# Row maxima ahead of the value and weight loads, fillers in two slots, second weight scale one slot later

## The chip, the cores and the metric

The kernel runs on one core of a Trainium2 chip. Its five engines work side by side, each through its own queue in order: TensorE (PE) multiplies matrices, VectorE (DVE) and ScalarE (ACT) work on elements, GpSimd (POOL) works on elements and issues DMAs, and SyncE (SP) issues DMAs. The metric is the device time of one execution in microseconds (us). The kernel before takes 1290.05 us in the median of three runs (1287.4 to 1290.46).

## The reference

The program is block-causal attention, and its output goes through a feed-forward layer with a gate.

```
scores = scale * np.matmul(q, k.transpose(0, 1, 3, 2))      # 8 x 8 heads of 576 x 64
scores = np.where(block_i >= block_j, scores, -1000000000.0)  # blocks of 64
attn = np.exp(scores - max); attn = attn / (sum + 1e-09)
x = (attn @ v).transpose(0, 2, 1, 3).reshape(4608, 512)
h = x @ w_in                                                 # 512 -> 2048
g = h * erf(softplus(h))
out = g @ w_out                                              # 2048 -> 512
```

## The kernel before

There are 64 heads, eight to a batch, and the program goes through them in slots (L648). Slot n makes the probabilities of head n (`probs`, L431: scores transposed as tile t, two matmuls to a piece, exponentials on ScalarE), the row maxima of head n + 2 (`maxes`, L387: scores as tile s on TensorE, six maxima on VectorE), and loads head n + 3 (`load_qk`, L371). The maxima of a head are turned on TensorE (tile mt, L424), copied by ScalarE and sent by a small DMA into one row of that head's `qk` tile (L427); the first matmul of the head's probabilities (L440) waits for that DMA. Every second slot multiplies the probabilities of two heads by v (`pv`, tile u) and sums their rows (tile us); every fourth slot normalises four heads (`normalise`) and sends the result x to memory.

`qk` takes four buffers. Each has five further rows with the mask, loaded once from `maskrows`. A head's load is three DMAs, two of them on POOL's queue and one on SP's, and then two subtractions on POOL (L382, L383) that make the low halves. The staging tile `st` of that load has two buffers.

The weights come as 64-bit floats, 32 half pieces of 512 KB, each 128 x 1024 words (`load_raw`, two buffers), and are converted by `to_f32`: two ScalarE passes and three VectorE passes a piece. Sixteen of the pieces are group 0 of the layer, sixteen are group 1. `TOF` says in which slots pieces are converted, `SCALE_AT` in which slot a group's scale is taken, and `SPLIT` in which slots its eight tiles are split into two half-precision parts. The layer's matmuls (m_h at L185 up, o at L194 down) begin when batch 0 is normalised, x has been read back and group 0 is split. From then on `moe1` gives out one step at a time, 12 a slot up to slot 19 and 28 a slot from slot 20.

Until the layer has read its first x, each slot also issues ten matmuls of a constant tile, whose result nobody reads (`warm`, L645): the fillers. Code order is not the final order. A scheduler places the instructions on each engine by priority, and the rows in the section on the change show what it made.

Of the kernel before, what the change touches and what calls it, by code (L numbers as in the profile page):

```python
# [23 lines left out]
def f32(ap):  # L24
    return ap.bitcast(F32)
# [7 lines left out]
def tile_attention_moe(ctx: ExitStack, tc: tile.TileContext, qk, v, w, maskrows, sels, out):  # L33
    nc = tc.nc
    B, H, D4, S = qk.shape
    D = D4 // 4
    NT, DM = out.shape
    NF = w.shape[0]
    P = 128
    NCC = DM // P  # L40
    SCALE = 0.125
    NQ = H // 4
# [19 lines left out]
    ident = cpool.tile([P, P], F32, name="ident")  # L62
    make_identity(nc, ident)
    ones32 = cpool.tile([P, 32], F16, name="ones32")
    nc.gpsimd.memset(ones32, 1.0)
    ones32t = cpool.tile([P, 32], F16, name="ones32t")
    nc.gpsimd.memset(ones32t, 0.0)
    nc.gpsimd.memset(ones32t[: S % P], 1.0)
    ones = cpool.tile([P, P], F32, name="ones")
    nc.gpsimd.memset(ones, 1.0)  # L70
# [35 lines left out]
    def load_raw(f, s, pool):  # L106
        raw = pool.tile([P, 2 * DM], I32, tag="raw", name=f"raw{f}_{s}", bufs=2)
        nc.sync.dma_start(raw, w[f, s].bitcast(I32))
        return raw.rearrange("p (n t) -> p n t", t=2)
# [179 lines left out]
    with tc.tile_pool(name="apool", bufs=2) as apool, tc.tile_pool(name="spool", bufs=1) as spool, \  # L289
# [5 lines left out]
        def memsets():  # L295
            nc.gpsimd.memset(pstage[0][64:128, 768:], 0.0)
            for t in rss:
                nc.gpsimd.memset(t[64:, S - SH :], 1.0)
            for t in mxs:
                nc.gpsimd.memset(t, 0.0)  # L300
# [13 lines left out]
        def load_v(b, qd):  # L314
            vt = apool.tile([P, 2, 4, 5, D], F16, tag="v", name=f"v{b}_{qd}")
            if b < B32:
                v32 = f32(vt.rearrange("p a b c d -> p (a b c d)")).rearrange("p (a b) -> p a b", a=4)
            else:
                v32 = apool.tile([P, 4, 5 * D], F32, tag="v32", name=f"v32_{b}_{qd}", bufs=1)
            nc.sync.dma_start(v32, v[b, :, 4 * qd : 4 * qd + 4, :])  # L320
            return v32, vt
# [257 lines left out]
        lows = []  # L579
        normals, ready_at, ready = {}, {}, 0  # L580
        for n in range(NB - 1):
            load, low = load_qk(n)
            if n == 2:
                for f in lows:
                    f()
                lows = []
            load()
            lows.append(low)
            nc.gpsimd.dma_start(qks[n][D : D + 5, 2 * S : 4 * S], maskrows)
            if n == 0:  # L590
                v32 = load_v(0, 0)
            if n == 1:
                memsets()
        nc.gpsimd.dma_start(qks[NB - 1][D : D + 5, 2 * S : 4 * S], maskrows)
        sel = spool.tile([P, 4], F32, name="sel")
        nc.sync.dma_start(sel, sels)
        for low in lows:
            low()
        scale_v(0, 0, *v32)
        vs[0] = prep_v(0, 0, *v32)  # L600
        rows = {}
        for n in range(2):
            *steps, rows[n] = maxes(n)
            for f in steps:
                f()
        rows.pop(0)()
# [11 lines left out]
        HALVES = [(f, i) for f in range(NF) for i in range(2)]  # L618
        TOF = {1: 2, 2: 2, 3: 2, 4: 2, 5: 2, 6: 2, 7: 2, 8: 2} | {n: 2 for n in range(11, 19)}
        SCALE_AT = {9: 0, 19: 1}  # L620
        SPLIT = {9: 2, 10: 3, 11: 3, 19: 2, 20: 2, 21: 2, 22: 2}
        raws = {}

        def next_raw():
            if len(raws) < len(HALVES):
                fs = HALVES[len(raws)]
                raws[fs] = load_raw(*fs, apool)

# [19 lines left out]
        for n in range(N + 3):  # L648
# [12 lines left out]
            qd = n // 4 + 1  # L661
            if n % 4 == 1 and qd < N // 4:
                v32 = load_v(*divmod(qd, NQ))
# [26 lines left out]
            if not loaded:  # L690
                lists.append(([warm] * WARM, 0, 1))
# [44 lines left out]
```

## Time and profile before

| | us |
|---|---|
| median of three runs | 1290.05 |
| the profiled execution | 1288.4 |
| its span | 1286.6 |
| TensorE busy | 1200.5 (93%) |
| VectorE busy | 895.8 (70%) |
| ScalarE busy | 780.5 (61%) |
| GpSimd busy | 523.6 (41%) |

The profile is one execution. Its page gives sums, and the trace behind it gives every instruction with its start, its duration, and the idle time before it with what ended it. Sums over the whole span say little of one stage: the first 165 us hold loads, conversions and attention alone, and after that the layer's matmuls fill TensorE. The granted clock is told as a share of full speed, 1.00 or 0.50 at any moment, so that 0.58 in a stretch is a mean of the two.

### The profile page before, as it was taken

What the parts mean: (1) busy time and instruction counts of PE and PEld (TensorE: products, weight loads), DVE (VectorE), ACT (ScalarE), POOL (GpSimd) and SP (SyncE); (2) the same over time, 40 slices, a digit from 0 to 9 for tenths busy, and PEclk for the clock granted to TensorE, in tenths of its full rate; (3) what the DMA queues carried; (4) which work ended last, traced back from release to release, by engine and by line L of the source; (5) the groups of instructions that cost most, each with busy time, mean ns of one, the idle gap of its engine ahead of it and who ended that gap; (6) DMA issues with size and microseconds to landing.
All of it is one profiled execution on the core that took longest, in us unless ns stands there. A gap on an engine that the chain in (4) does not pass through costs nothing.

```text
span 1286.6 us, 23640 instructions
## 1 busy us (share of the span) xinstructions
PE 1200.5 (93%) x9108; PEld 810.2 (63%) x9108; DVE 895.8 (70%) x1583; ACT 780.5 (61%) x1555; POOL 523.6 (41%) x488
## 2 busy tenths in 40 slices
PE   1899999989999999999999999999999999999997
PEld 0455566556666666767667666766667667666664
DVE  3853689887567878688777778795777765555554
ACT  2453567667556666766666756666666775555553
POOL 4444435553435453545445344544445331321221
PEclk9887889989999999999999999999999999999999
DMA  9794566862454554453545444554444221221111
GB/s 250 210 218 97 125 170 172 229 148 67 109 122 121 135 133 110 105 143 114 110 114 124 111 109 128 131 122 100 115 112 113 63 69 52 82 66 50 53 63 50
DMA packets 95808, 151.74 MB, mean 118 GB/s; under 512 B 7804, under 2 KB 44988, under 8 KB 95696
## 3 DMA queue, kind: packets, MB, share of 16 engines
q1 hardware_dynamic: 69840, 93.34, 24.4%
q0 software_dynamic: 25216, 56.73, 21.5%
q8 instruction: 72, 1.18, 0.4%
q14 instruction: 40, 0.33, 0.1%
q10 hardware_dynamic: 640, 0.17, 0.1%
HBM read 121.73 MB, written 28.31 MB: 117 GB/s over the span
## 4 chain that ended last, share of the span: by engine, by line
PE 49%; DVE 26%; ACT 14%; DMA 5%; issue 4%; POOL 1%; SPq 0%; DVEq 0%; POOLq 0%; ACTq 0%
PE m_h L185 14%; PE o L194 14%; DVE m_r L158 5%; DVE m_r L157 5%; PE u L489 4%; DVE m_r L159 4%; DVE m_r L160 3%; PE t L440 3%; ACT m_r L155 3%; ACT m_r L154 3%; PE s L394 3%; ACT m_r L156 3%; PE t L441 3%; DVE mx L397 2%; PE us L512 2%
## 5 line engine op out<-in xcount | busy, mean ns | idle before, releaser
L185 PE MATMUL m_h<-xh,w 128*128 128x256 f16 x2304 | 476.9, 276 | 12.8 <-DVE m_r L160 12.5
L185 PEld LDWEIGHTS <-w 128*128 128x128 f16 x3456 | 326.7, 99 | 146.6 <-issue 24.1
L194 PE MATMUL o<-w,m_gh 128*128 128x512 f16 x1152 | 337.0, 382 | 10.5 <-DVE pt L235 6.4
L162 POOL TENSOR_TENSOR m_gl<-m_r,m_gh 128x512 f16<-128x512 f32 x144 | 174.3, 1211 | 403.6 <-ACT m_gh L161 362.8
L185 PE MATMUL m_h<-xl,w 128*128 128x256 f16 x1152 | 316.6, 275 | 0.0
L397 DVE TENSOR_REDUCE mx<-s 64x1 f32<-64x288 f32 (+4 forms) x384 | 174.8, 470 | 110.8 <-PE s L394 109.8
L157 DVE SCALAR_TENSOR_TENSOR m_r<-m_r 128x512 f32<-128x512 f32 x144 | 115.6, 803 | 171.1 <-ACT m_r L156 168.9
L445 ACT ACTIVATE p<-t 128x288 f32<-128x288 f32 (+4 forms) x384 | 146.0, 385 | 108.7 <-PE t L441 102.7
L194 PE MATMUL o<-w,m_gl 128*128 128x512 f16 x576 | 206.0, 384 | 0.3 <-POOL m_gl L162 0.3
L161 ACT CAST m_gh<-m_r 128x512 f16<-128x512 f32 x144 | 88.8, 617 | 192.0 <-DVE m_r L160 187.9
L440 PE MATMUL t<-qk 69*128 69x288 f32 (+4 forms) x384 | 168.0, 438 | 13.1 <-DMA qk<-mt 7.5
L394 PE MATMUL s<-qk 68*64 68x288 f32 (+3 forms) x384 | 150.9, 424 | 27.4 <-DVE mx L397 14.9
L382 POOL TENSOR_TENSOR qk<-st,qk 64x576 fp32r<-64x576 f32 x64 | 95.9, 1498 | 149.4 <-DMA qk<-qk 136.2
L154 ACT ACTIVATE m_r<-m_h,c,bs 128x512 f32<-128x512 f32 (+3 forms) x192 | 124.1, 666 | 45.1 <-PE m_h L185 43.0
L194 PEld LDWEIGHTS <-m_gh 128*128 128x128 f16 x1152 | 98.5, 98 | 67.2 <-issue 19.7
L158 DVE SCALAR_TENSOR_TENSOR m_r<-m_r,m_r 128x512 f32<-128x512 f32 x144 | 120.6, 837 | 2.8
L441 PE MATMUL t<-qk 128*128 128x288 f32 (+4 forms) x384 | 120.1, 313 | 0.0
L159 DVE SCALAR_TENSOR_TENSOR m_r<-m_r 128x512 f32<-128x512 f32 x144 | 115.7, 803 | 2.9
L383 POOL TENSOR_TENSOR qk<-st,qk 64x576 fp32r<-64x576 f32 x64 | 103.1, 1611 | 30.0 <-DMA qk<-qk 27.1
L457 DVE TENSOR_TENSOR p<-p,p 128x832 f16<-128x832 f32 x80 | 82.6, 1033 | 36.3 <-ACT p L456 36.2
L156 ACT ACTIVATE m_r<-m_r,c 128x512 f32<-128x512 f32 x144 | 103.7, 720 | 2.9 <-ACT m_r L155 0.8
L155 ACT ACTIVATE m_r<-m_r,c 128x512 f32<-128x512 f32 x144 | 103.8, 721 | 1.7
(98 smaller groups left out, 1484.9 us busy)
## 6 DMA issues: line engine op xcount, KB each, us to landing
qk<-qk POOLq DMA_DIRECT2D x64, 432.0 KB, 5.0
st<-qk SPq DMA_DIRECT2D x64, 288.0 KB
qk<-qk POOLq DMA_DIRECT2D x64, 288.0 KB, 5.2
raw<-w SPq DMA_DIRECT2D x32, 512.0 KB
v<-v SPq DMA_DIRECT2D x16, 640.0 KB
x_d<-xs POOLq DMA_DIRECT2D x32, 288.0 KB, 3.5
xh<-x_d SPq DMA_DIRECT2D x36, 256.0 KB
xl<-x_d SPq DMA_DIRECT2D x36, 256.0 KB
```

Source lines behind the costliest of these rows:

```text
L154: nc.scalar.activation(r0s[:, :, lo:hi], h[:, :, lo:hi], AF.Tanh, bias=const(p1), scale=bss[b][g][:, 0:1])
L157: nc.vector.scalar_tensor_tensor(out=r0, in0=r0, scalar=c3, in1=r0, op0=ALU.add, op1=ALU.mult)
L158: nc.vector.scalar_tensor_tensor(out=r0, in0=r1, scalar=c4, in1=r0, op0=ALU.add, op1=ALU.mult)
L159: nc.vector.scalar_tensor_tensor(out=r0, in0=r0, scalar=c5, in1=r0, op0=ALU.add, op1=ALU.mult)
L162: nc.gpsimd.tensor_tensor(out=gl, in0=r0, in1=gh, op=ALU.subtract)
L185: nc.tensor.matmul(h[:, k, :], lhsT=wf[:, a, sl], rhs=x[:, cc, :], start=cc == 0 and i == 0, stop=cc == NCC - 1 and i == 2)
L194: nc.tensor.matmul(o[c], lhsT=a[:, sl], rhs=wf[:, b_, :], start=u == u0 and k == 0 and not lo and b_ == 2, stop=u == u1 - 1 and k == nu - ...
L394: nc.tensor.matmul(dst[:r, :w_], lhsT=qh[:K, i * P : i * P + r], rhs=kh[:K, k0 : k0 + w_], start=True, stop=True)
L397: nc.vector.tensor_reduce(out=mx[:r, col : col + 1], in_=src, axis=AX.X, op=ALU.max, negate=True)
L440: nc.tensor.matmul(s[:kk, :w_], lhsT=kh[:K, ks], rhs=qh[:K, q0 : q0 + w_], start=True, stop=False)
L441: nc.tensor.matmul(s[:kk, :w_], lhsT=klh[:, ks], rhs=qhl[:, q0 : q0 + w_], start=False, stop=True)
L445: nc.scalar.activation(p32s[part][:kk, c : c + w_ - skip], s[:kk, skip:w_], AF.Exp, scale=SCALE)
```

## The change

- The mask rows are loaded once from memory, first on POOL's queue, and copied into the other three buffers by DMAs on ScalarE's queue. Their masked value is -2^100 in place of -1e30.
- Heads 0 to 2 are loaded next. The constants are set after head 1's load has been issued, the memsets after head 2's.
- The first load of v, and the loads of the first weight pieces, now wait: VectorE writes one element from the row maxima into the target tile, and the load, which overwrites that element, stands behind it. Later loads of v have such a copy too.
- The first v is scaled in slots 0 and 1. One piece of weights is converted in each of slots 0 and 1, then two a slot up to slot 8 as before.
- Fillers stand in slots 0 and 1 alone.
- The second scale is taken in slot 20 in place of 19, and the eight tiles of group 1 are split in slots 20 to 23 in place of 19 to 22.

```
+        if src is not None:
+            nc.vector.tensor_copy(f32(raw[:1, :1]), src)
         nc.sync.dma_start(raw, w[f, s].bitcast(I32))
...
+            nc.vector.tensor_copy(v32[:1, 0, :1], src)
             nc.sync.dma_start(v32, v[b, :, 4 * qd : 4 * qd + 4, :])
...
+        heads = [load_qk(n) for n in range(NB - 1)]
+        masks = [qks[n][D : D + 5, 2 * S : 4 * S] for n in range(NB)]
+        nc.gpsimd.dma_start(masks[0], maskrows)
+        for m in masks[1:]:
+            nc.scalar.dma_start(f32(m), f32(masks[0]))
+        heads[0][0]()
         sel = spool.tile([P, 4], F32, name="sel")
         nc.sync.dma_start(sel, sels)
+        heads[1][0]()
+        constants()
+        heads[2][0]()
+        memsets()
+        for _, low in heads:
             low()
-        scale_v(0, 0, *v32)
-        vs[0] = prep_v(0, 0, *v32)
...
         for n in range(2):
             *steps, rows[n] = maxes(n)
             for f in steps:
                 f()
-        rows.pop(0)()
+            if n == 0:
+                v32 = load_v(0, 0, mxs[0][:1, 3:4])
+                rows.pop(0)()
+            next_raw(mxs[n][:1, 3:4])
...
-        TOF = {1: 2, 2: 2, 3: 2, 4: 2, 5: 2, 6: 2, 7: 2, 8: 2} | {n: 2 for n in range(11, 19)}
-        SCALE_AT = {9: 0, 19: 1}
-        SPLIT = {9: 2, 10: 3, 11: 3, 19: 2, 20: 2, 21: 2, 22: 2}
+        TOF = {0: 1, 1: 1, 2: 2, 3: 2, 4: 2, 5: 2, 6: 2, 7: 2, 8: 2} | {n: 2 for n in range(11, 19)}
+        SCALE_AT = {9: 0, 20: 1}
+        SPLIT = {9: 2, 10: 3, 11: 3, 20: 2, 21: 2, 22: 2, 23: 2}
...
+            if n < 2:
+                lists.append(([lambda v0=v32: scale_v(0, 0, *v0), lambda v0=v32: vs.__setitem__(0, prep_v(0, 0, *v0))][n : n + 1], 0.6, 0.8))
             if n % 4 == 1 and qd < N // 4:
-                v32 = load_v(*divmod(qd, NQ))
+                v32 = load_v(*divmod(qd, NQ), mxs[(n + 1) % 2][:1, 3:4])
...
-            if not loaded:
+            if n < 2:
                 lists.append(([warm] * WARM, 0, 1))
...
-        maskrows[j, 1, 128 * j : 128 * j + 64] = -1e30
+        maskrows[j, 1, 128 * j : 128 * j + 64] = -(2.0**100)
```

VectorE at the start of the program, before: its first maxima (mx, from the scores s of heads 0 and 1) stand behind the conversion of the first pieces of weights (w from raw, the pieces of tiles 1 and 2 shown).

```order
L116 TENSOR_SCALAR w_99<-raw_0_371 128x512
L117 SCALAR_TENSOR_TENSOR w_99<-a_0_478,w_99 128x512
L118 SCALAR_TENSOR_TENSOR w_99<-a_0_478,w_99 128x512
L116 TENSOR_SCALAR w_99<-raw_1_484 128x512
L117 SCALAR_TENSOR_TENSOR w_99<-a_1_486,w_99 128x512
L118 SCALAR_TENSOR_TENSOR w_99<-a_1_486,w_99 128x512
L116 TENSOR_SCALAR w_100<-raw_0_492 128x512
L117 SCALAR_TENSOR_TENSOR w_100<-a_0_575,w_100 128x512
L116 TENSOR_SCALAR w_100<-raw_1_581 128x512
L397 TENSOR_REDUCE mx_152<-s_0_207 128x1 x2
```

VectorE at the same place now, from its first instruction on:

```order
L403 TENSOR_REDUCE mx_144<-s_0_200 128x1 x2
L403 TENSOR_REDUCE mx_144<-s_0_205 128x1
L403 TENSOR_REDUCE mx_144<-s_0_208 128x1
L403 TENSOR_REDUCE mx_144<-s_0_0_211 64x1
L403 TENSOR_REDUCE mx_144<-s_0_1_214 64x1
L325 COPY v_0_217<-mx_144 1x1
L112 COPY raw_0_226<-mx_144 1x1
L428 TENSOR_REDUCE mx_144<-mx_144 64x1
```

The maxima of head 0 are VectorE's first work, and the two copies behind them release the loads of v and of the first piece of weights.

SP's queue at the start, before (st: a head's staging tile, v, raw: a piece of weights):

```order
L378 DMA st_170<-qk 128x576
L320 DMA v_0_175<-v 128x1280
L378 DMA st_177<-qk 128x576
L596 DMA sel<-sels 128x4
L320 DMA v_1_316<-v 128x1280
L108 DMA raw_0_355<-w 128x1024
L108 DMA raw_1_363<-w 128x1024
L320 DMA v_3_0_3154<-v 128x1280
L108 DMA raw_0_371<-w 128x1024
L108 DMA raw_1_484<-w 128x1024
```

SP's queue at the start now:

```order
L384 DMA st_162<-qk 128x576
L593 DMA sel<-sels 128x4
L384 DMA st_163<-qk 128x576
L384 DMA st_164<-qk 128x576
L384 DMA st_250<-qk 128x576
L326 DMA v_0_217<-v 128x1280
L113 DMA raw_0_226<-w 128x1024
L113 DMA raw_1_246<-w 128x1024
L384 DMA st_326<-qk 128x576
L113 DMA raw_0_375<-w 128x1024
```

Four heads' staging loads now stand ahead of v, and pieces of weights alternate with heads.

TensorE in slot 7, before (t: probabilities of head 7, s: scores of head 9, mt: maxima of head 8, warm: the fillers):

```order
L440 MATMUL t_7_0_992<-qk_137 128x288
L441 MATMUL t_7_0_992<-qk_137 128x288
L394 MATMUL s_9_996<-qk_135 128x256 x2
L645 LDWEIGHTS ones_82
L645 MATMUL warm<-ones_82 32x512
L440 MATMUL t_7_288_1002<-qk_137 128x288
L441 MATMUL t_7_288_1002<-qk_137 128x288
L645 LDWEIGHTS ones_82
L645 MATMUL warm<-ones_82 32x512
L394 MATMUL s_9_1007<-qk_135 128x384
L424 MATMUL mt_1011<-ident,mx_152 5x128
```

TensorE in slot 7 now:

```order
L446 MATMUL t_7_0_946<-qk_129 128x288
L447 MATMUL t_7_0_946<-qk_129 128x288
L400 MATMUL s_9_950<-qk_127 128x256 x2
L446 MATMUL t_7_288_955<-qk_129 128x288
L447 MATMUL t_7_288_955<-qk_129 128x288
L400 MATMUL s_9_959<-qk_127 128x384
L446 MATMUL t_7_128_1000<-qk_129 128x448
L447 MATMUL t_7_128_1000<-qk_129 128x448
L400 MATMUL s_9_0_997<-qk_127 64x288
L446 MATMUL t_7_256_1007<-qk_129 128x320
L430 MATMUL mt_963<-ident,mx_144 5x128
```

The fillers are gone, and the maxima of head 8 are turned a few matmuls later in the slot.

## Rows read from the trace of the kernel before

**Rows 1.** The page, 40 slices of the span: granted clock in tenths, GB/s.

```profile
PEclk9887889989999999999999999999999999999999
GB/s 250 210 218 97 125 170 172 229 148 67 109 122 121 135 133 110 105 143 114 110 114 124 111 109 128 131 122 100 115 112 113 63 69 52 82 66 50 53 63 50
```

**Rows 2.** Stretches: length, busy us by engine (instructions), granted clock, DMA share, GB/s.

```profile
10.00:20.00 10.00, 1.99 (x6) 1.36 (x6) 3.52 (x6) 1.33 (x2) 3.72 (x3) 1.00 1.18 294
60.00:70.00 10.00, 9.93 (x85) 5.80 (x83) 6.92 (x21) 7.05 (x20) 3.70 (x4) 0.95 1.04 234
100.00:110.00 10.00, 10.00 (x37) 5.66 (x39) 3.00 (x8) 3.32 (x8) 6.26 (x7) 0.50 0.61 158
150.00:160.00 10.00, 7.40 (x60) 4.33 (x58) 9.97 (x17) 7.09 (x15) 8.30 (x8) 0.83 0.52 134
280.00:300.00 20.00, 16.98 (x121) 11.49 (x122) 19.25 (x36) 14.48 (x31) 7.94 (x7) 0.83 0.35 88
...
165.00:290.00 125.00, 112.42 (x818) 75.84 (x818) 110.68 (x210) 84.23 (x195) 62.27 (x54) 0.93 0.69 177
290.00:1068.00 778.00, 759.17 (x6188) 531.68 (x6187) 577.02 (x1006) 513.41 (x1009) 341.58 (x304) 1.00 0.45 112
```

**Rows 3.** Timeline of DVE at the start: start, us, what, [idle before <- releaser].

```profile
30.42 0.43 DVE L116 TENSOR_SCALAR w<-raw 128x512 int32<-128x512 int32 x1 [2.88 <-DMA raw<-w]
...
32.06 4.72 DVE L397 TENSOR_REDUCE mx<-s 128x1 f32<-128x128 f32 x12
```

**Rows 4.** Timeline of PE at the start.

```profile
13.52 1.99 PE L394 MATMUL s<-qk 68*128 68x256 f32 x6 [6.29 <-DMA qk<-maskrows]
...
38.15 0.27 PE L424 MATMUL mt<-ident,mx 128*5 128x128 f32 x1
38.36 3.63 PE L645 MATMUL warm<-ones 128*32 128x512 f16 x16
41.91 0.40 PE L440 MATMUL t<-qk 69*128 69x288 f32 x1
```

**Rows 5.** Timeline of POOL, the first load that it issues.

```profile
1.68 0.77 POOL L377 DMA_DIRECT2D qk<-qk  x1
```

**Rows 6.** The page's DMA issues: queue, count, KB each, median us to landing.

```profile
qk<-qk POOLq DMA_DIRECT2D x64, 432.0 KB, 5.0
st<-qk SPq DMA_DIRECT2D x64, 288.0 KB
qk<-qk POOLq DMA_DIRECT2D x64, 288.0 KB, 5.2
raw<-w SPq DMA_DIRECT2D x32, 512.0 KB
v<-v SPq DMA_DIRECT2D x16, 640.0 KB
```

**Rows 7.** The chain of waits in slots 2 to 4: start, us, what.

```profile
64.18 7.35 DMA qk<-mt
...
74.90 5.37 DMA qk<-mt
```

**Rows 8.** Groups by line, PE, first 165 us: busy us, mean ns, idle before.

```profile
L645 PE MATMUL warm<-ones 128*32 128x512 f16 x110 | 39.3, 453 | 0.0
```

**Rows 9.** Timeline of PE in slots 5 to 7: first t of head 5, a filler, head 7.

```profile
88.56 0.30 PE L440 MATMUL t<-qk 69*128 69x288 f32 x1
...
106.98 0.61 PE L645 MATMUL warm<-ones 128*32 128x512 f16 x1
...
118.40 0.40 PE L440 MATMUL t<-qk 69*128 69x288 f32 x1
```

**Rows 10.** Timeline of PE: first t of head 9, first matmul of the layer.

```profile
138.05 0.40 PE L440 MATMUL t<-qk 69*128 69x288 f32 x1
...
164.91 0.39 PE L185 MATMUL m_h<-xh,w 128*128 128x256 f16 x2
```

**Rows 11.** Timeline of PE in slot 19, behind the second scale and split.

```profile
284.41 0.63 PE L440 MATMUL t<-qk 69*128 69x320 f32 x1 [1.82 <-DVE mx L397]
```

More of the change, by code (lines that the diff above doesn't have):

```diff
@@ L62, in tile_attention_moe, with constants @@
     ident = cpool.tile([P, P], F32, name="ident")
-    make_identity(nc, ident)
     ones32 = cpool.tile([P, 32], F16, name="ones32")
-    nc.gpsimd.memset(ones32, 1.0)
     ones32t = cpool.tile([P, 32], F16, name="ones32t")
-    nc.gpsimd.memset(ones32t, 0.0)
-    nc.gpsimd.memset(ones32t[: S % P], 1.0)
     ones = cpool.tile([P, P], F32, name="ones")
-    nc.gpsimd.memset(ones, 1.0)
+    def constants():
+        make_identity(nc, ident)
+        nc.gpsimd.memset(ones32, 1.0)
+        nc.gpsimd.memset(ones32t, 0.0)
+        nc.gpsimd.memset(ones32t[: S % P], 1.0)
+        nc.gpsimd.memset(ones, 1.0)
     bias = {}
@@ L104, in powers, with load_raw @@
         nc.vector.tensor_scalar(out=i32(inv), in0=i32(inv), scalar1=23, scalar2=None, op0=ALU.logical_shift_left)
-    def load_raw(f, s, pool):
+    def load_raw(f, s, pool, src):
         raw = pool.tile([P, 2 * DM], I32, tag="raw", name=f"raw{f}_{s}", bufs=2)
+        if src is not None:
+            nc.vector.tensor_copy(f32(raw[:1, :1]), src)
         nc.sync.dma_start(raw, w[f, s].bitcast(I32))
@@ L312, in bank, with load_v @@
             return ps_a.tile([P, 512], F32, tag="a", name=name)
-        def load_v(b, qd):
+        def load_v(b, qd, src):
             vt = apool.tile([P, 2, 4, 5, D], F16, tag="v", name=f"v{b}_{qd}")
@@ L578, in tile_attention_moe, with next_raw @@
         vs, prs, usbs = {}, {}, {}
-        lows = []
         normals, ready_at, ready = {}, {}, 0
[L581 to L594, printed above, removed]
+        heads = [load_qk(n) for n in range(NB - 1)]
[4 more added lines that the diff above has]
+        heads[0][0]()
         sel = spool.tile([P, 4], F32, name="sel")
         nc.sync.dma_start(sel, sels)
-        for low in lows:
+        heads[1][0]()
[3 more added lines that the diff above has]
+        for _, low in heads:
             low()
-        scale_v(0, 0, *v32)
-        vs[0] = prep_v(0, 0, *v32)
         rows = {}
+        HALVES = [(f, i) for f in range(NF) for i in range(2)]
+        raws = {}
+        def next_raw(src=None):
+            if len(raws) < len(HALVES):
+                fs = HALVES[len(raws)]
+                raws[fs] = load_raw(*fs, apool, src)
         for n in range(2):
@@ L617, in tile_attention_moe @@
         LQ = 0.1
-        HALVES = [(f, i) for f in range(NF) for i in range(2)]
-        TOF = {1: 2, 2: 2, 3: 2, 4: 2, 5: 2, 6: 2, 7: 2, 8: 2} | {n: 2 for n in range(11, 19)}
-        SCALE_AT = {9: 0, 19: 1}
-        SPLIT = {9: 2, 10: 3, 11: 3, 19: 2, 20: 2, 21: 2, 22: 2}
[L622 to L627, printed above, removed]
+        TOF = {0: 1, 1: 1, 2: 2, 3: 2, 4: 2, 5: 2, 6: 2, 7: 2, 8: 2} | {n: 2 for n in range(11, 19)}
+        SCALE_AT = {9: 0, 20: 1}
+        SPLIT = {9: 2, 10: 3, 11: 3, 20: 2, 21: 2, 22: 2, 23: 2}
         def conv():
```

## The prediction, made before the changed kernel was run

> **What bounds the kernel now.** I read the page's slices first, then sums by stretch, then the timelines of VectorE and TensorE up to the first matmul of the layer, and the chain of waits there. The span falls into three stages. From 290 to 1068 us TensorE is busy 759 of 778 us at a granted clock of 1.00 [rows 2]: what is left to do at 290 us is a fixed amount of TensorE work, and whatever comes earlier at its start comes earlier at its end. From 165 to 290 us VectorE is busiest, 110.7 of 125 us, and the stage waits in turn on it and on TensorE [rows 2]. Before 165 us no layer matmul has run (the first starts at 164.91 [rows 10]). The page's slices show its first three at 250, 210 and 218 GB/s and the fourth at 97, and the granted clock below 9 tenths nowhere but in its slices up to the ninth [rows 1]. This opening is what the change rewrites, so the question is when that first matmul will start.
>
> The opening has three parts. First, the scores of head 0 are done on TensorE from 13.52 us [rows 4], but VectorE takes the maxima only at 32.06 us, since its queue still holds conversions, the last of which starts when a piece of weights lands at 30.42 us [rows 3]. The first probability matmul (t of head 0) is at 41.91 us [rows 4]. Second, from there to t of head 9 at 138.05 us [rows 10] nine slots take 96.1 us, 10.7 each. While weights are loading the DMAs are saturated: share 1.04 at 234 GB/s from 60 to 70 us [rows 2], and a DMA of one row of maxima, a few KB, needs 7.35 and 5.37 us and ends the longest waits [rows 7]. Once the weights are in, TensorE sets the pace, 10.00 of 10 us at a clock of 0.50 from 100 to 110 us [rows 2], with fillers in between. Third, from t of head 9 to the first layer matmul are 26.9 us, in which VectorE is full with splitting weights, 9.97 of 10 us from 150 on [rows 2].
>
> **The change part by part.** Start. Five loads of POOL (the mask, heads 0 and 1) and the first of head 2 come to 22.5 + 2 x (432 + 288 + 288) + 432 KB, the staging tiles on SP's queue counted in [rows 6], or 2.53 MB. At 294 GB/s, the best ten microseconds of the trace [rows 2], that is 8.6 us after an issue at about 1.7 us [rows 5], so 10.3 us. Head 0's maxima then wait for nothing but its scores and the memsets. But on TensorE the turn of head 0's maxima stands behind head 2's first scores, so it comes at 10.5 us and not earlier. Behind it come the DMA of the row, 3.8 us from turn to t [rows 4], and on TensorE seven score matmuls and thirteen fillers, at 0.23 us each when fast (3.63 us for sixteen [rows 4]) and 0.61 when slow [rows 9]: 3 to 8 us, and about 2 for the scores. I take 7.5 us for what is longer of the two, and t of head 0 at 18 us. Bounds: 15 (DMA alone) and 22. The part is worth 41.9 - 18 = 23.9 us. The constants and memsets that were moved are hidden under the loads. The mask copies on ScalarE's queue wait for the first mask alone, and ScalarE has nothing else to do then.
>
> Slots 0 to 8. A slot's head is 432 + 288 + 288 KB, its two pieces of weights 1024 KB, its share of v 160 KB [rows 6]: 2.245 MB, or 9.6 us at 234 GB/s. In slots 0 and 1 one piece is missing, but v is loaded there whole, and by the hold all of it comes after the heads. So nine slots take 86.4 us, and t of head 9 is at 18 + 86.4 = 104.4 us; the part is worth 96.1 - 86.4 = 9.7 us. The fillers removed (110 in all, 39.3 us of TensorE [rows 8], of which twenty remain) lie under the DMAs in slots 2 to 4 and are bare afterwards. What takes their place as the latest is the load. From below, the same bytes at 294 GB/s are 7.6 us a slot; from above, see the first rival. Held loads of v add a copy on VectorE in sixteen slots, next to nothing each, but each waits for the old v to be read; what queues behind it on VectorE are maxima. From 290 us on VectorE is busy 577 of 778 us [rows 2], and that slack covers a microsecond a time. Bare, it would cost up to sixteen times that.
>
> To the first layer matmul. In slots 9 and 10 twenty fillers go, ten a slot, 9.1 us at 0.453 [rows 8]. VectorE's splits hide about half (9.97 of 10 us [rows 2]), so I take 4 us, 23 us in place of 26.9. Bounds 0 and 8. The first layer matmul comes at 127.4 us, 37.5 earlier.
>
> Second scale. In slot 19 TensorE waits for VectorE, 1.82 us in one place [rows 11], and 280 to 300 us has 3.0 us idle and a clock of 0.83 [rows 2], that is 6.8 us at the low level, which cost 3.4. Relief can gain 7 us, or the same stall can come in slot 20. On the other side, by the rates of the code four layer steps in slot 23 find no split weights and are done at the end, about 3 us. I take 0. The mask's new value changes no instruction's time.
>
> Sum: 23.9 + 9.7 + 4 + 0 = 37.6 us off the profiled execution's own 1288.4 us (span 1286.6), 1250.8. The median of the runs is 1.65 above that execution: 1252 us.
>
> **The rivals.** (1) TensorE's clock stays low without fillers, and TensorE paces slots 2 to 8. For it: from 100 to 110 us the clock was 0.50, the lower of its two levels, with TensorE 10.00 of 10 us busy [rows 2], and six of the first nine slices are below 9 tenths [rows 1]. From the first t of head 5 at 88.56 to that of head 7 at 118.40 us nineteen fillers ran (a count of such rows), a third of that time surely at the low level; less 19 x 0.61 us [rows 9] that leaves 9.1 us a slot. With some 2 us of waits for a row of maxima, 11.1 a slot: t of head 9 at 118, the first layer matmul at 143 with 2 us saved behind it, 22 us gained, 1268 us. Against it: 9.1 is still under the DMA's 9.6, so the low level need not show.
>
> The Trainium skill, page "TensorE: Matmul & The Clock Gate", section "Part 1: The HAM clock gate", says that the throttled clock is the default and that activity releases it, which speaks for this rival. Only in part does the trace agree: the stretch at 0.50 above was fully busy, with fillers.
>
> (2) The DMAs do better than 234 GB/s once loads are spread evenly. At 294, 7.6 us a slot, t of head 9 comes at 87 us and the first layer matmul at 110: 55 us gained, 1235 us. For it: 10 to 20 us did so [rows 2]. Against: those were mostly weights, and the mix of slots 2 to 4 gave 234.
>
> The Trainium skill, page "HBM Reference", section "Specifications (TRN2)", gives about 358 GB/s to a core. By that a slot would take 6.3 us. No ten microseconds of this trace show it, and the measured rates decide.
>
> (3) No change: the hold gives the start back. If each of the eight pairs of weight pieces took 15.4 us from issue to its second conversion, group 0 would be ready at 14 + 8 x 15.4 = 137 us as t of head 9 is now, and nothing would be left. The first load of a head takes 5.0 us to land in the median [rows 6], so this needs a chain three times as long.
>
> (4) Slower: the clock stays low beyond the opening, in slots 11 to 19, where TensorE is busy 112.4 of 125 us at 0.93 [rows 2]. A stretch at the low level costs up to half its length, so 75 us of low level there would eat the 37.6 us, and all 125 would add some 60 less what VectorE hides, 1275 to 1315 us. Against it: after the last filler the clock came back each time (0.93 over the stage, about 17 us low).
>
> **How the numbers follow.** The forecast has a chance of 0.50 (1242 to 1262 by itself), rival 1 has 0.23, rival 2 0.18, rival 3 0.04, rival 4 0.05. The range leaves out rival 4, the far half of rival 2 and the worst of rival 1 (t of head 9 at 122): 1232 to 1272. Within 0.3% (4 us), about what a measurement of this kernel can tell from no change, falls rival 3: 0.04. Slower is rival 4: 0.05. Faster is the rest, 0.91.
>
> **What would show it.** In the profile after: VectorE's first maxima near 8 us in place of 32.06, t of head 0 at 15 to 22 us, DMA share near 1 from 20 to 90 us, t of head 9 at 95 to 112, the first layer matmul at 120 to 135, and from there the same spacing as before to the end. A clock at 0.5 with TensorE full from 30 to 100 us would show rival 1. I am wrong if slots 2 to 8 take over 11 us, or if the stage from the first layer matmul to the end grows by more than 8 us.

## The result

The changed kernel takes 1278.47 us in the median of six runs (1272.52 to 1282.6), the kernel before beside it 1290.26: a ratio of 0.990, interval 0.987 to 0.993. Run again beside later experiments it took 1275.7, ratio 0.990 (0.984 to 0.995). It is faster by 12 to 17 us. The ratios here and below are those of fast runs and not the quotients of the medians, from which they differ by up to 0.004. The forecast was 1252, 38 us faster: the direction is right, a third to less than half of the gain is there, and the time lies outside the range.

### The profile page after: what moved, and what is told of

Read it like the earlier page. It is cut to its first block, busy times and chain, and to the rows that moved or that the text cites. A ratio compares the mean times of both kernels' runs of the same rounds, so it can differ in the third digit from the quotient of the medians.

```text
span 1276.7 us, 23450 instructions
## 1 busy us (share of the span) xinstructions
PE 1179.3 (92%) x9018; PEld 804.2 (63%) x9018; DVE 893.6 (70%) x1601; ACT 776.0 (61%) x1555; POOL 524.4 (41%) x485
## 4 chain that ended last, share of the span: by engine, by line
PE 41%; DVE 28%; ACT 16%; DMA 7%; issue 5%; POOL 2%; DVEq 0%; SPq 0%; POOLq 0%; ACTq 0%
PE m_h L190 13%; PE o L199 12%; DVE m_r L163 5%; DVE m_r L162 5%; DVE m_r L164 5%; PE u L495 4%; DVE m_r L165 4%; ACT m_r L161 3%; ACT m_r L159 3%; ACT m_r L160 3%; DMA qk<-qk 3%; PE us L518 3%; PE t L446 2%; DVE mx L403 2%; PE s L400 2%
## 5 line engine op out<-in xcount | busy, mean ns | idle before, releaser
L190 PE MATMUL m_h<-xh,w 128*128 128x256 f16 x2304 | 474.2, 275 | 10.3 <-DVE m_r L165 8.4
L162 DVE SCALAR_TENSOR_TENSOR m_r<-m_r 128x512 f32<-128x512 f32 x144 | 113.1, 785 | 195.4 <-ACT m_r L161 185.7
L446 PE MATMUL t<-qk 69*128 69x288 f32 (+4 forms) x384 | 168.2, 439 | 11.1 <-DMA qk<-mt 5.8
L164 DVE SCALAR_TENSOR_TENSOR m_r<-m_r 128x512 f32<-128x512 f32 x144 | 115.0, 798 | 2.6
```

Source lines behind the costliest of these rows:

```text
L162: nc.vector.scalar_tensor_tensor(out=r0, in0=r0, scalar=c3, in1=r0, op0=ALU.add, op1=ALU.mult)
L164: nc.vector.scalar_tensor_tensor(out=r0, in0=r0, scalar=c5, in1=r0, op0=ALU.add, op1=ALU.mult)
L190: nc.tensor.matmul(h[:, k, :], lhsT=wf[:, a, sl], rhs=x[:, cc, :], start=cc == 0 and i == 0, stop=cc == NCC - 1 and i == 2)
L446: nc.tensor.matmul(s[:kk, :w_], lhsT=kh[:K, ks], rhs=qh[:K, q0 : q0 + w_], start=True, stop=False)
```

## The profile after

The profiled execution takes 1278.48 us (span 1276.7). In what follows a slot begins with the first exponential of its head. First the page's slices, to hold against [rows 1]:

```profile
PEclk9876799989999999999999999999999999999999
...
GB/s 220 236 193 185 148 163 203 192 107 104 117 121 125 123 98 128 126 117 135 99 126 106 135 108 128 103 123 119 104 120 111 53 77 60 60 72 45 59 58 50
```

A slice is 32 us. The transfers that were crowded into the first three now reach over four: the fourth carries 185 GB/s in place of 97. In it the clock is at six tenths. The stretches, with the columns of [rows 2]:

```profile
0.00:10.00 10.00, 1.89 (x6) 1.36 (x6) 1.01 (x4) 1.28 (x1) 8.36 (x29) 1.00 1.00 187
10.00:20.00 10.00, 6.23 (x17) 2.70 (x17) 4.85 (x18) 0.26 (x1) 6.71 (x6) 1.00 1.36 224
...
70.00:80.00 10.00, 7.80 (x23) 4.32 (x24) 7.36 (x15) 3.88 (x9) 4.36 (x3) 0.50 0.83 184
100.00:110.00 10.00, 6.50 (x25) 3.81 (x29) 3.02 (x9) 2.47 (x6) 3.74 (x4) 0.50 1.16 214
165.00:290.00 125.00, 111.78 (x837) 73.53 (x837) 99.15 (x200) 79.13 (x190) 61.20 (x53) 0.96 0.68 167
290.00:1068.00 778.00, 757.21 (x6206) 530.99 (x6205) 575.89 (x1014) 513.33 (x1008) 337.12 (x302) 1.00 0.45 112
```

From 290 us on hardly anything differs. From 70 to 80 us TensorE is at the lower of its two levels, 7.80 of 10 us busy, with no fillers about; from 100 to 110 us it is again at 0.50, 6.50 us busy where [rows 2] has 10.00. Next the start, on VectorE (to [rows 3]) and TensorE (to [rows 4]):

```profile
8.99 2.41 DVE L403 TENSOR_REDUCE mx<-s 128x1 f32<-128x128 f32 x6 [8.99 <-PE s L400]
...
13.36 0.81 DVE L403 TENSOR_REDUCE mx<-s 64x1 f32<-64x288 f32 x2 [1.79 <-PE s L400]
```

```profile
8.11 1.99 PE L400 MATMUL s<-qk 68*128 68x256 f32 x6 [8.11 <-DMA qk<-qk]
...
15.55 0.55 PE L400 MATMUL s<-qk 68*128 68x256 f32 x1 [1.33 <-DMA qk<-qk]
15.90 0.41 PE L430 MATMUL mt<-ident,mx 128*5 128x128 f32 x1
...
19.75 3.21 PE L647 MATMUL warm<-ones 128*32 128x512 f16 x10
23.36 0.37 PE L446 MATMUL t<-qk 69*128 69x288 f32 x1 [0.39 <-DMA qk<-mt]
...
115.88 0.37 PE L446 MATMUL t<-qk 69*128 69x288 f32 x1
...
143.34 0.39 PE L190 MATMUL m_h<-xh,w 128*128 128x256 f16 x2
```

The maxima start at 8.99 us, as forecast. The turn of the row (mt) comes at 15.90, behind a wait for head 2's load at 15.55, and t of head 0 at 23.36. The last two lines answer to [rows 10]: t of head 9 at 115.88, the first layer matmul at 143.34. Against [rows 4, 10] the gain is 18.6 us at t of head 0, 22.2 at t of head 9, 21.6 at the first layer matmul, and 9.9 at the end of the span.

## The experiments

Their ratios are to the kernel before, run beside them. Places, in us, of the profiles that the text compares:

| kernel | slot 0 | slot 5 | slot 9 | first m_h | slot 14 | end |
|---|---|---|---|---|---|---|
| before | 43.7 | 89.1 | 138.6 | 164.9 | 210.7 | 1286.6 |
| before, second profile | 44.6 | 90.2 | 131.0 | 155.6 | 201.3 | 1288.5 |
| before, third profile | 44.7 | 90.5 | 137.1 | 163.3 | 209.1 | 1289.0 |
| after | 24.6 | 67.7 | 116.4 | 143.3 | 193.2 | 1276.7 |
| after, second profile | 27.7 | 72.0 | 123.2 | 149.5 | 200.0 | 1285.2 |
| fillers back everywhere | 25.8 | 77.7 | 125.7 | 151.9 | 197.7 | 1284.4 |
| fillers in 0, 1, 5 to 10 | 25.7 | 66.5 | 108.6 | 135.9 | 183.2 | 1268.4 |
| new order alone | 27.6 | 70.9 | 117.0 | 143.3 | 187.1 | 1274.9 |
| before, fillers cut | 44.2 | 86.9 | 127.0 | 148.4 | 197.2 | 1280.1 |

**Clock or transfers.** Four kernels ask what sets slots 2 to 8.

```diff
-            if n < 2:
+            if not loaded:                # all fillers back
+            if n < 2 or n > 4 and not loaded:   # another kernel: fillers late
```

All fillers back: 

> The changed kernel with the fillers back in every slot until the layer reads its input (ten a slot in slots 0 to 10, 110 instead of 20). Theory A (clock): the opening fell 12 us short of the forecast because TensorE, without fillers, runs at its low clock: 20.5 us of low clock lie between t of head 9 and the first layer matmul, where the kernel before had 6.8. With the fillers that low clock goes: t of head 9 about 3 to 5 us earlier than 116.4, the first layer matmul 6 to 10 us earlier than 143.3, total 1268 to 1273 us. Theory B (transfers: heads and pieces of weights arrive too slowly, TensorE waits at any clock): first layer matmul within 3 us of 143.3, total 1275 to 1281. If the fillers are bare, as the forecast had it for slots 9 and 10, the total grows by 4 us or more.

Measured: 1291.3 us, ratio 1.004 (1.001 to 1.008); the whole gain is gone. The first layer matmul comes 8.6 us later, 7.6 of it from slots 2 to 4. Here they are, and then the same slots of the changed kernel:

```profile
41.90:77.70 35.80, 32.77 (x187) 15.96 (x187) 22.69 (x52) 17.79 (x49) 13.01 (x12) 0.82 0.77 178
```

```profile
39.50:67.70 28.20, 23.92 (x172) 14.04 (x172) 19.51 (x47) 15.93 (x45) 14.77 (x13) 0.89 0.97 226
```

Theory A's numbers failed: with fillers in every slot the clock is no higher there, and TensorE has 8.9 us more to do. That is not a price of the fillers as such: the new order alone, below, has them in these slots too and takes 24.7 us.

Fillers late: 

> The changed kernel with ten fillers a slot in slots 0, 1 and 5 to 10, none in 2 to 4. With fillers in all of them slots 2 to 4 had grown by 7.6 us, slots 5 to 8 stayed at 48 (low clock 13.7 in place of 27.3 us, idle 1.7 in place of 10.7) and slots 9 and 10 at 26. Theory A (the low clock of slots 5 to 10 is worth something once fillers stand only there): first layer matmul 3 to 8 us earlier than 143.3, total 1270 to 1275. Theory F (fillers give back what they take, wherever they stand): first layer matmul within 2 us of 143.3, total 1276 to 1282.

Measured: 1272.4 us, 0.985 (0.982 to 0.989), the first layer matmul 7.4 us earlier. Slots 5 to 8 of the changed kernel, and then of this one:

```profile
67.70:116.40 48.70, 38.01 (x223) 23.07 (x223) 31.36 (x65) 24.12 (x66) 22.94 (x21) 0.72 0.83 195
```

```profile
66.50:108.60 42.10, 36.64 (x249) 22.13 (x248) 28.91 (x64) 23.96 (x66) 19.89 (x19) 0.92 0.99 227
```

Twenty-six more instructions take 1.4 us less of TensorE, and its idle time falls from 10.7 to 5.5 us. At two levels of 0.5 and 1, a mean of 0.72 is 27 of 48.7 us at the low one, 0.92 is 7 of 42.1. This is what theory A forecast. Other profiles bear it out in the main: the four kernels with fillers late and also in slots 0 and 1 take 41.6 to 42.6 us in slots 5 to 8, at 0.92; the changed kernel in both profiles, and the four of its variants that touch only v, x or the second scale, take 47.6 to 51.2, at 0.67 to 0.76. With fillers in every slot it is 48.0 us at 0.86 (46.1 at 0.93 in the new order alone), and two kernels of the start, below, do not fit. So fillers late shortened these slots of this kernel by about 6 us; that the clock alone did it is not shown, and in the total the interval and the changed kernel's overlap.

A quarter of the weights, and a quarter of the heads:

```diff
-        nc.sync.dma_start(raw, w[f, s].bitcast(I32))
+        nc.sync.dma_start(raw[:, : DM // 2], w[f, s].bitcast(I32)[:, : DM // 2])
...
-                nc.gpsimd.dma_start(t[:D, 1:4, :], ...)
+                nc.gpsimd.dma_start(t[:D, 1:4, :m], ...)   # another kernel: m = S // 4 for heads 4 to 11
```

> The changed kernel with only the first quarter of every piece of weights loaded (128 KB in place of 512) and read four times over by the conversions, so that every instruction but the load stays; the weights are therefore not the reference's. Theory B (transfers): in slots 0 to 8 the bytes of a slot fall from 2.245 to 1.48 MB, so with the DMAs as the bound a slot takes 6.3 to 7 us in place of 10.2, t of head 9 comes 20 to 28 us earlier than 116.4 and the total is 1250 to 1258. Theory A (clock, or TensorE and VectorE work): slots 2 to 8 stay within 1 us of their length, t of head 9 within 6 us, total 1272 to 1279.

> The changed kernel with heads 4 to 11 loading only the first quarter of their columns (252 KB in place of 1008 in three DMAs); their scores are then computed on what the buffer held before, so these heads are not the reference's. Every other instruction stays. Theory L (what sets slots 2 to 8 is the loop through the four buffers: last read of a buffer, 7 to 9 us of load, the subtraction on POOL, scores): the loads take 2 to 4 us, TensorE's 9.0 us of waits for them between 40 and 116 us go, and the low clock that follows each of them; t of head 9 comes 12 to 20 us earlier than 116.4, total 1260 to 1268. Theory A (TensorE's work at a clock that stays low without fillers, whatever the loads do): t of head 9 within 5 us of 116.4 less the 9 us of waits at most, low clock in slots 5 to 8 still over 20 us, total 1270 to 1278.

Measured: 1271.9 us, 0.988 (0.983 to 0.994), slot 9 at 114.1; and 1269.3, 0.982 (0.977 to 0.987), slot 9 at 110.6. Slots 5 to 8 of the first and of the second:

```profile
69.10:114.10 45.00, 36.68 (x218) 21.89 (x216) 29.89 (x63) 23.13 (x66) 20.07 (x21) 0.73 0.68 150
```

```profile
65.10:110.60 45.50, 37.15 (x217) 22.92 (x217) 26.59 (x60) 23.27 (x66) 22.64 (x19) 0.70 0.46 146
```

With the DMA share down from 0.83 to 0.68 and 0.46 the slots are 3 to 4 us shorter, and TensorE stays at 0.70 to 0.73. Slots 2 to 4, where the changed kernel's share was 0.97, take 28.9 and 28.3 us at shares of 0.56 and 0.53, in place of 28.2. Theories B and L, which wanted t of head 9 at least 20 and 12 us earlier, are wrong: slot 9 comes 2.3 and 5.8 earlier. Each kernel leaves the other kind of load whole; both cut at once were not run. TensorE's waits for loads of heads in the changed kernel, 40 to 116 us (in all, times, longest), are 9 us:

```profile
PE s L400 <- DMA qk<-qk: 9.0, 3, 7.0
PE t L446 <- DMA qk<-mt: 3.4, 2, 2.5
```

In slots 5 to 8 they are 8.7 of its 10.7 us of idle time. When the loads of heads got quick, other waits took their place, the longest of them 4.6 us for ScalarE:

```profile
PE s L409 <- ACT mt L441: 4.6, 1, 4.6
```

**The parts alone.** The kernel before with only the fillers cut (`if n < 2` in place of `if not loaded`): 

> The kernel before with the one edit that fillers stand in slots 0 and 1 alone (20 in place of 110). Theory A (without fillers the clock stays low in slots 5 to 10, and that costs what the fillers cost): low clock in slots 5 to 8 and up to the first layer matmul over 40 us, where the kernel before has 27.3, t of head 9 within 6 us of 138.6, total 1284 to 1292. The forecast's step (the fillers are bare once the weights are in: 40 of them in slots 5 to 8, 20 in slots 9 and 10): t of head 9 8 us or more earlier, total 1276 to 1282.

Measured: 1284.2 us, 0.996 (0.993 to 1.000). Slots 5 to 8:

```profile
86.90:127.00 40.10, 37.51 (x223) 24.46 (x222) 15.06 (x38) 15.29 (x42) 21.18 (x22) 0.70 0.62 130
```

Both are half right: slot 9 comes early, as the forecast's step says, and the clock is 0.70 and the total 1284, as theory A says. The stretch is shorter than in two profiles of the kernel before (49.5 and 46.6 us), not than in the other (40.8). The 223 instructions need about 38 us at this clock, here and in the changed kernel; the changed kernel has 10.7 us of idle on top, with VectorE at 31.4 us in place of 15.1. The change moved work there: of the first eighteen pieces of weights, the kernel before begins to convert eight before slot 0 and none in slots 5 to 8, the changed kernel one and eight.

The new order alone (`if not loaded`, `SCALE_AT = {9: 0, 19: 1}` with its splits, later loads of v with no copy ahead): 

> The changed kernel with the other three parts undone: fillers in every slot until the layer reads x, the second scale in slots 19 to 22, the hold kept for the first v and the first two pieces of weights alone. What is left is the new order of the opening. Theory S (the parts add: the start is worth 18 us, the fillers in slots 2 to 4 take back 7.6, the rest is neutral): t of head 0 at 24 to 27 us, the first layer matmul at 150 to 154, total 1277 to 1281. Theory V (the holds on the later loads of v shape the order behind the opening and leaving them out costs 10 us, as it did when they alone were undone): 1287 to 1294, with slot 14 to the end at 1090 us or more in place of 1083.5.

Measured: 1279.3 us, 0.991 (0.987 to 0.995), theory S's total, but not its sum: the first layer matmul is at 143.3, where it wanted 150 to 154. Slots 2 to 4, with the fillers in them:

```profile
46.20:70.90 24.70, 24.30 (x188) 14.28 (x187) 22.46 (x51) 16.97 (x47) 10.66 (x11) 1.00 0.78 217
```

The 7.6 us that the fillers cost above are not there. The order alone has about the gain of the whole change; the other three parts come out near nothing together, within the 5 us or so that the intervals leave open.

The later loads of v without a hold:

```diff
-                v32 = load_v(*divmod(qd, NQ), mxs[(n + 1) % 2][:1, 3:4])
+                v32 = load_v(*divmod(qd, NQ), None)
```

> The changed kernel with the hold on the loads of v kept for the first one alone; the other fifteen start as soon as their buffer is free. Theory D (held loads of v come late: VectorE waited 2.33 us for one at 123 us and TensorE 5.73 us behind it, and there are fifteen): first layer matmul 4 to 7 us earlier than 143.3, total 1270 to 1275. Rival (what waited for v would have waited for the next load of a head anyway): total within 3 us of 1278.5.

Measured: 1290.7 us, 1.003 (0.999 to 1.006): a miss. The first layer matmul stays (142.9), and slot 14 to the end takes 1095.0 us where the changed kernel has 1083.5. Theory D and its rival both failed. Left out together with the other parts, in the kernel above, the hold is not missed (theory V wanted 1287 to 1294). Why it is when it alone goes is open; the effects of the parts do not add.

**Behind the first layer matmul.** The second scale:

```diff
-        SCALE_AT = {9: 0, 20: 1}
+        SCALE_AT = {9: 0, 19: 1}
```

> The changed kernel with the second scale and its splits put back to slots 19 to 22. Theory C (the second scale in slot 20 costs what was lost after slot 19: four layer steps find no weights, and slots 20 to 30 grew by 9 us against the spacing before): total 1270 to 1274, with slots 24 to 29 some 4 us shorter; the first layer matmul stays at 143. Rival (that loss comes from elsewhere, from the clock or the held loads of v): total within 3 us of 1278.5.

Measured: 1274.0 us, 0.991 (0.987 to 0.995), within the spread of the changed kernel (0.990): not told apart. What its profile showed, as that of the changed kernel does, is a stall in slot 19. The changed kernel's waits there, the issues of x on SP's queue, and the next head's on POOL:

```profile
PE m_h L190 <- DMA xl<-x_d: 4.6, 1, 4.6
PE m_h L190 <- DMA xh<-x_d: 1.7, 1, 1.7
```

```profile
252.69 0.37 SPq L222 DMA_DIRECT2D xh<-x_d  x1
253.11 0.50 SPq L222 DMA_DIRECT2D xl<-x_d  x1
```

```profile
253.09 0.64 POOL L383 DMA_DIRECT2D qk<-qk  x1 [0.94 <-PE t L447]
```

x and the next head are issued at the same moment, and TensorE waits 6.3 us. In the first profile of before the head came 2.6 us after x, and it did not wait:

```profile
268.95 0.37 SPq L217 DMA_DIRECT2D xh<-x_d  x1
```

```profile
271.53 0.64 POOL L377 DMA_DIRECT2D qk<-qk  x1 [3.11 <-PE t L441]
```

x loaded by ScalarE (`nc.scalar.dma_start(x, ...)`), then also with the second scale in slot 19, then with fillers late:

> The changed kernel with the loads of the layer's input x (xh, xl) issued by ScalarE in place of SyncE. In the changed kernel TensorE waits 6.3 us in slot 19 for x, whose loads are issued at 252.69 and 253.11 us, behind a staging load on SP's queue and at the same moment as the next head's loads, and land 9.03 us later; the clock is low for 10.2 us there. Theory E (this wait is the new loss behind the first layer matmul): x is issued some 3 to 5 us earlier, the wait in slot 19 falls under 2 us and the low clock there goes; slot 19 falls from 19.8 to 11 to 13 us, total 1268 to 1273. Rival (the order of the work around slots 19 to 24 costs it, whatever x does): total within 3 us of 1278.5. If ScalarE stands waiting for x to be written before it can issue, its exponentials come late and the total grows.

> The changed kernel with both edits: x loaded by ScalarE and the second scale back in slots 19 to 22. Theory E plus theory C (each takes away a loss of its own): total 1264 to 1269. Rival (both touch the same stall in slot 19, which either alone removes): no better than the better of the two alone, 1270 to 1274.

> The changed kernel with ten fillers a slot in slots 0, 1 and 5 to 10 (alone 1272.4) and x loaded by ScalarE (alone 1276.3, with the wait for x in slot 19 gone). If the wait for x is worth its 7 us and the clock behind it, 1262 to 1268. If what it holds up there is made up for by work that would otherwise come later, as the 1276.3 alone suggests, 1270 to 1274.

Measured: 1276.3 (0.987, 0.983 to 0.991), 1274.3 (0.987, 0.983 to 0.991) and 1274.3 us (0.989, 0.985 to 0.992). The wait is gone (0.3 us for x in the first), but the time stays: theory E's 1268 to 1273 failed, and with fillers late it is no better than fillers late alone. Against the three kernels without this edit the ratios differ by -0.003, -0.004 and +0.004, where 6.3 us would be -0.005; a small gain can't be excluded. That what is held up in slot 19 is made up later is likely, and not shown. The kernel before again, twice: 

> The kernel before, profiled again. Theory W (the wait for x in slot 19 is a matter of when the opening ends and hits the kernel before as well in some executions): a gap of TensorE before m_h in slot 19 of 4 us or more in one of the two profiles, slot 14 to the end 1080 to 1086 there. Theory N (the change brings it): no such gap in either, the next head's loads 2 to 3 us after x's, slot 14 to the end 1074 to 1078.

> The kernel before, profiled a third time; the same expectations as for the second.

Measured: 1290.3 and 1290.8 us. Both show the gap, theory W (6.9 and 6.5 us). Over all twenty profiles it goes by the two issues: in the thirteen where x and the next head are issued within half a microsecond of each other, TensorE waits 5.6 to 7.5 us for x in slot 19; in the seven where the head comes 2.3 to 3.1 us later, 1.2 at most. The second profile's wait for x, and then slot 14 to the end in the three profiles of before (each a fence) and in the changed kernel:

```profile
PE m_h L185 <- DMA xh<-x_d: 5.1, 1, 5.1
...
PE m_h L185 <- DMA xl<-x_d: 1.8, 1, 1.8
```

```profile
210.70:1286.60 1075.90, 1033.24 (x8121) 712.40 (x8118) 764.25 (x1312) 679.03 (x1312) 430.69 (x382) 0.99 0.42 106
```

```profile
201.30:1288.50 1087.20, 1037.62 (x8121) 714.49 (x8120) 763.84 (x1312) 679.17 (x1312) 430.77 (x383) 0.99 0.41 105
```

```profile
209.10:1289.00 1079.90, 1031.69 (x8121) 711.94 (x8120) 761.84 (x1312) 679.50 (x1312) 431.83 (x383) 0.99 0.41 106
```

```profile
193.20:1276.70 1083.50, 1032.42 (x8121) 711.78 (x8119) 759.56 (x1323) 676.97 (x1312) 429.46 (x382) 0.99 0.42 106
```

The same 8121 matmuls take 1076 to 1087 us in one and the same kernel; the changed one lies between. The second profile of the changed kernel: 

> The changed kernel once more, unaltered, beside the kernel before and the three others of this set: 1275 to 1281 us. If its first layer matmul and its slot 14 stand within 3 us of 143.3 and 193.2, differences of 5 us and more between profiles of the other kernels are differences of the kernels.

Measured: 1275.7 us in the median, but its profiled execution was the slowest of six (1287.0), with the first layer matmul at 149.5 and slot 14 at 200.0. Places in single profiles of one kernel differ by 7 us and more, so a smaller difference between two profiles carries nothing here unless several kernels repeat it.

**The start.** Weights held until a probability of head 0 is there; then with fillers late; then also without the fillers of slots 0 and 1:

```diff
-            next_raw(mxs[n][:1, 3:4])
...
+            if n == 0:
+                lists.append(([lambda: next_raw(prs[0][0][0][:1, :1])] * 2, 0.8, 1))
```

> The changed kernel with the first two pieces of weights held until a probability of head 0 is there, instead of until its maxima are taken (their conversions start in slot 1 instead of 0, two a slot). Theory T (in the changed kernel the row of maxima of head 0 took 6.3 us because weights and v were loading beside it): 3.5 to 4.5 us for the row, t of head 0 at 20 to 22.5 us. Rival (TensorE's turn, behind the scores of head 2, sets it): t of head 0 within 1 us of 23.4. The total: 1273 to 1282, since conversions come later by the same 5 to 10 us.

> The changed kernel with ten fillers a slot in slots 0, 1 and 5 to 10 (alone 1272.4) and the first two pieces of weights held until a probability of head 0 is there (alone 1271.4). Fillers late gained in slots 5 to 8 (42.1 in place of 48.7 us) through the clock, weights later in slots 0 and 1 (12.7 in place of 14.9) and by the luck of slot 19. If they add: t of head 9 at 103 to 107, the first layer matmul at 130 to 134, total 1265 to 1269. If both repair the same clock: first layer matmul at 135 to 137, total 1270 to 1274.

> The same without the fillers of slots 0 and 1: ten a slot in slots 5 to 10 alone. Theory Q (TensorE's own queue sets t of head 0, thirteen fillers of 4.08 us right before it): t of head 0 at 20 to 21.5 us, and 2 to 4 us off the opening, total 1262 to 1268. Theory A (the clock needs them): TensorE's clock is low already in slots 0 to 2, which then take 4 us or more longer, and the total is no better than with them.

Measured: 1271.4 us (0.988, 0.984 to 0.992), 1269.9 (0.983, 0.978 to 0.988) and 1276.9 (0.986, 0.981 to 0.991). TensorE before t of head 0 in the first, and then in the third, with ScalarE's issue of the row:

```profile
19.72 4.08 PE L646 MATMUL warm<-ones 128*32 128x512 f16 x13
23.73 0.40 PE L446 MATMUL t<-qk 69*128 69x288 f32 x1
```

```profile
24.45 0.58 PE L446 MATMUL t<-qk 69*128 69x288 f32 x1 [5.71 <-DMA qk<-mt]
```

```profile
17.89 0.70 ACTq L433 DMA_DIRECT2D qk<-mt  x1
```

And the same issue in the changed kernel:

```profile
16.64 0.71 ACTq L433 DMA_DIRECT2D qk<-mt  x1
```

In the first, fillers stand right before t and it waits for nothing; without them, in the third, it waits 5.71 us for the row, which takes 6.6 us from issue to t with the weights out of the way (the DMAs moved 196 GB/s there), as it took 6.7 with them (298 GB/s). Theory T is wrong for the weights; the load of v stayed beside the row, and a row with no load beside it was not run. Theory Q is wrong too: row and fillers end together, and taking one away leaves the other. Theory A's clock did not fall in the third: slots 0 and 1 run at 1.00 without a filler. Slots 5 to 8, without fillers in the first and with them in the third, are the two that do not fit above:

```profile
69.30:111.10 41.80, 34.59 (x222) 21.29 (x221) 30.45 (x63) 23.92 (x66) 24.39 (x21) 0.84 0.95 237
```

```profile
68.20:116.50 48.30, 45.00 (x260) 24.15 (x259) 32.26 (x67) 24.25 (x66) 22.23 (x21) 0.86 0.83 209
```

With both edits, weights later and fillers late, the time is 1269.9 us, the lowest median of the kernels that load everything (1264.7 to 1275.5; the changed kernel's twelve runs lie between 1271.7 and 1287.0), but its first layer matmul (137.9) does not show that the two add, and its interval and the changed kernel's overlap.

Fillers late with the second scale in slots 19 to 22: 

> The changed kernel with the two edits that each made it faster by themselves: ten fillers a slot in slots 0, 1 and 5 to 10 (alone 1272.4), second scale in slots 19 to 22 (alone 1274.0). If they act in different places, opening and slots 20 to 24, they add: 1266 to 1269 us, first layer matmul at 134 to 138. If what either gains in one profile is no more than the spread between runs, 1272 to 1276.

Measured: 1272.0 us, 0.985 (0.980 to 0.990): no more than fillers late alone.

## Why the prediction was wrong

The sum had 37.6 us, and the profile gained 9.9. Of the 27.7 between them, 5.3 are the start, 6.1 slots 0 to 8, 4.6 the stretch to the first layer matmul and 11.7 the rest.

**Start, forecast 23.9 us, measured 18.6.** The mechanism is right and the size of one term is off: TensorE's turn was put at 10.5 us, by 2.53 MB at 294 GB/s. It came at 15.9: up to 15.5 us the DMAs moved 198 GB/s in the mean, which makes about 3.1 MB, so both the rate and the bytes that came first were off. (Nor was 294 the best of the trace of before, which moved 313 from 12 to 22 us.) The other term, 7.5 us from turn to t, measured 23.36 - 15.90 = 7.5, with some luck: its share for the row alone (3.8 us) did not hold, over 6.

**Slots 0 to 8, forecast 9.7 us, measured 3.6** (t of head 0 to t of head 9: 92.5 in place of 96.1). This is the step that failed in kind. It took the DMAs for the bound, 9.6 us a slot. Slots 2 to 4 took just that, 9.4 us at a share of 0.97, but no less at half the share. Slots 5 to 8 took 12.2 us a slot at a mean clock of 0.72 and a DMA share of 0.83: 9.5 of TensorE's work at this clock and 2.7 of idle time. With fillers late they took 42.1 us, with a quarter of the weights 45.0, with a quarter of the heads 45.5. Rival 1 had this mechanism. Its places are right within about 2 us (t of head 9 at 118, first layer matmul at 143) with luck, since it began at 18 us, 5 too early, and its 11.1 us a slot were 10.3; its total, 1268, missed what follows below. The argument held against it, that 9.1 us of TensorE a slot lie under 9.6 of DMA, left out TensorE's idle time, 10.7 us in slots 5 to 8, which comes on top of its work and does not lie beside it. Nor are the 9.1 sound: eight of the nineteen fillers, all put at 0.61 us, took 0.39 or less in that trace, and with their own durations TensorE has 10.0 us a slot, over the 9.6. The low clock alone does not explain the 12.2 either: the kernel before with its fillers cut does the same work at 0.70 in 10.0 us a slot. Where the idle time of the changed kernel comes from is not shown; what it has in these slots, and the kernel before has not, are eight pieces of weights with their loads and conversions.

The Trainium skill, page "TensorE: Matmul & The Clock Gate", section "Part 1: The HAM clock gate", says that the throttled clock is the default and that activity releases it; the pair of 0.72 without and 0.92 with fillers agrees, and the kernel before, at 0.79 in its first profile without a gap on TensorE, does not. How much the level is worth, this kernel shows best, slots 5 to 8 in its second profile and in its first:

```profile
90.20:131.00 40.80, 40.80 (x262) 22.00 (x260) 16.22 (x41) 15.73 (x44) 22.63 (x23) 1.00 0.71 147
```

```profile
89.10:138.60 49.50, 49.50 (x262) 25.80 (x260) 16.32 (x41) 16.03 (x43) 22.65 (x23) 0.79 0.55 121
```

The same 262 instructions took 8.7 us longer where the clock was at 0.50 for part of them. So the profile that the forecast was made from had itself the slowest opening of the three, by 9 and 2 us at the first layer matmul.

**To the first layer matmul, forecast 4 us, measured -0.6.** Fillers were taken out of slots 9 and 10 and nothing was gained: the stretch is 26.9 us from slot 9 in the changed kernel (clock 0.62), 26.2 with all fillers back (0.87). With the same 26 us at either clock, TensorE does not set it; VectorE, full with splits from 150 us on in [rows 2], is the likely bound (not tested), and then all of the fillers lay beside it, not half. In the one profile of the kernel before with its fillers cut the stretch is 21.4 us, in place of 24.6 to 26.3; there their removal seems to bring what was forecast.

**From there to the end, forecast 0, measured 11.7 lost.** The step "same spacing" failed twice. The marker moved: in the changed kernel the first layer matmul runs 9.3 us before slot 11 begins (152.6), before 0.6 us after it, so 4.0 us of the 11.7 are gone by slot 14, where the layer has run equally far (130 or 131 matmuls m_h since its start). The other 7.6 us are a difference to one profile of before, the shortest rest of the three (1075.9, 1079.9, 1087.2). Over three profiles before and two after, slot 14 comes at 207.0 and 196.6, and the rest is 1081 and 1084: the gain was made in the opening, about 10 us by these profiles, and little is lost behind it. The second scale (forecast 0) could not be told from no change.

Point by point of what was to show it: maxima near 8 us, yes; t of head 0 at 15 to 22, missed by 1.4; DMA share near 1 from 20 to 90, not from 40 to 50 (0.74) and not from 70 on; t of head 9 at 95 to 112, missed by 4; first layer matmul at 120 to 135, missed by 8. Of the two bounds for "I am wrong", the rest (8 us) was crossed, and slots 2 to 8 came out at it: 76.9 us, 11.0 a slot.

Open stay the cost of leaving out the held loads of v alone, why removing the wait for x gives nothing back, and why fillers in the same slots cost 7.6 us in one kernel and nothing in another.

## What to carry to other kernels

Before a rate from the best ten microseconds of a trace, or the rest of a kernel behind a marker, goes into a sum as a constant, profile the same kernel again: here the opening and the rest each moved by ten microseconds between executions that agreed in the total. Fillers are neither bare cost nor free: put back everywhere they took the whole gain, 13 us, and put back in slots 5 to 10 but not 2 to 4 they shortened slots 5 to 8 by about 6. But what they did in one place changed with the kernel around them (slots 2 to 4: 35.8 and 24.7 us), so price them by the median of many runs and not from one stretch. When a load, a row or a filler is on the path, look what ends just beside it before pricing its removal.

## What was not expected of the hardware

The same stretch of one program, slots 5 to 8 of the kernel before, was granted a clock of 1.00 in one execution and 0.79 in another, with TensorE busy without a gap in both (40.8 and 49.5 us). A DMA of one row of maxima, 2.5 KB, took 6.6 us with a megabyte of weights out of its way, and 6.7 with it (the load of v ran in both). And whether two loads are issued within half a microsecond or 2.3 us apart and more went, in all twenty profiles, with a wait of 5.6 to 7.5 us or of at most 1.2, and showed no clear effect on the time of the kernel.
